# One more V tile kept between two attention layers, and the places at the change of layers dealt anew

## The chip, the core and the metric

The kernel runs on one core of a Trainium2 chip. The metric is the device time of one execution in microseconds (us). The engines named here: PE (matrix products), DVE (vector), ACT (activations), POOL (small extra vector work), SP (issues the loads), and the sixteen DMA engines that move the data. "1 MiB", "512 KB" and "256 KB" are sizes of one transfer; a tile of 1 MiB is 8 KB in each of the 128 partitions of the on-chip memory, and a *place* is half of a tile, 4 KB per partition.

## What is computed

Two identical rounds of attention and GLU for four single tokens, with the same weights and the same caches in both rounds:

```python
x = x + attn(layernorm(x), k_cache, v_cache, wq, wo)
x = x + glu(layernorm(x), w_gate, w_up, w_down)
x = x + attn(layernorm(x), k_cache, v_cache, wq, wo)
x = x + glu(layernorm(x), w_gate, w_up, w_down)

# attn: q = (x @ wq) in 32 heads of 128; 8 heads of K and V, last 2048 positions
#   p = softmax(q @ k.T * 128**-0.5); o = p @ v; return o @ wo
# glu: (sigmoid(x @ w_gate) * (x @ w_up)) @ w_down, 512 -> 1792 -> 512
```

Batch 4, width 512, everything bfloat16. K and V of the window have 16 MiB each, `wq` and `wo` 4 MiB each, the three GLU matrices 1.75 MiB each. The K cache stays on the chip after its first use; most of V and the weights except `wo` are read from HBM once per round.

## The kernel before, in words

**Memory.** One big array, `arena`, has 50 slots of 4 KB per partition. The first 32 hold K of all eight heads for the whole run. The other 18 are nine tiles of two slots, given out by a pool. V comes in 16 tiles of 1 MiB, one for each of 8 heads and each pair `bp` of batches. `wo` takes four tiles and stays until the second attention. So at the end of the first attention five tiles are left. Names in the code: `Y` = first V tile of head 7, `Z` = second V tile of head 7, `GA` = first V tile of head 6, `GB` = a pair of slots without content of its own. The fifth is the second V tile of head 6.

**What stays.** V of heads 7 and 6 is used last in the first attention and first in the second, where the heads run backwards. `Z` and the second tile of head 6 simply stay. `Y` is copied into four PSUM banks by four DVE transposes of 128x512 (`st0` to `st3`, line 574) and comes back by four transposes (`us0` to `us3`, line 589) into a tile that the second attention has freed. Half of `Z` goes to two more PSUM banks (`so0`, `so1`, line 596) and comes back into its place (`uo0`, `uo1`, line 602). Of `GA` one half stays (`KEPT`), the other half is loaded again.

**The ring of places.** At the change of layers the first GLU's weights (`wg`, `wu`: four transfers of 448 KB each; `wd`: three of 512 KB and one of 256 KB), then `wq` for the second attention (eight of 512 KB), then three V halves of 512 KB pass through six places: `GB` 0 and 1, `GA` 0, `Y` 0 and 1, `Z` 0. Each load names its place in a table written by hand (in `load_wq`, `load_glu`, `load_v`). A load waits until the matmul, or the transposes, that read the place before it have ended.

**Order.** The loads are issued by SP strictly in the order of the list `loads`; a load that waits holds up all behind it. For the other engines `_schedule` orders the operations before the run with a cost model: of those that could start within 60 ns of the earliest it takes the one written first. Each operation has the dependences that follow from what it reads and writes, from the PSUM banks it shares, and from explicit `after` and `deps`. From the second `wq` product on (`P.chain`) PE keeps the program's order.

**Units.** In the first attention, for each head: K is transposed in place (line 847), scores, softmax, probabilities transposed, two products with V (`pv_unit`, line 966), the rescaling `oe` (line 974), a permutation `pm` on PE (984), `oq` (989), and the product with `wo` (`wo_unit`, 1153), which adds up in PSUM bank `WB` over all heads. Then `attn_add` (1278) reduces that bank to the new x, and `layer_norm` (740 and following) begins with a sum over x (`ln_red`), a product that makes the mean (`ln_sum`), and the centred x (`ln_xn`). `glu` (1290) multiplies the `wg` and `wu` parts as they land (1330), transposes (1339), makes `hT` (1357) and multiplies the `wd` parts (1396). `q_second` and `q_mms` (788) do the second `wq` product in two halves (`i` = 1, then 0); the result of the first half is transposed (`qt1_1`, 800) and scaled (`qc1_1`, 804), and then unit 0 of the second attention starts with `qx2.0` (835) and its scores (865, 876). In the last GLU (`last=True`) the `wd` products are at line 1371, and four copies `oc0` to `oc3` (1382), by turns on ACT and DVE, bring the result into `ebuf`, from where it is stored.

## Time and profile before

| | us |
|---|---|
| median of three runs | 180.24 (179.0 to 181.01) |
| the profiled execution | 179.2 |
| its span, first to last instruction | 177.5 |
| busy: PE / DVE / ACT / POOL | 101.9 / 104.0 / 32.7 / 21.6 |
| DMA: bytes, mean rate over the span | 70.26 MB, 396 GB/s |
| V loads | 27 of 1 MiB, 3 of 512 KB |
| SP waiting for V products of line 966 | 27.5, in 8 waits |

Times in what follows are us from the first instruction of the span. In a row of a group or of the timeline the columns are start, length, engine, line, operation, what is written and read with partitions x elements, the count, and in brackets the idle time of the engine before it and what ended that. The chain that ended last goes back from the last instruction to what released each step. "DMA to landing" is the time from the start of an issue on SP until all sixteen engines have reported that transfer.

### The profile page before, as it was taken

To read this page: it belongs to the slowest core of one execution; us is meant where nothing else is said; L and a number is where in the kernel's file an instruction comes from. 1 tells how busy PE (TensorE), PEld (TensorE's weight loads), DVE (VectorE), ACT (ScalarE), POOL (GpSimd) and SP (SyncE) were. 2 spreads that over 40 slices of the span, in tenths; PEclk is the share of its full clock that TensorE was granted. 3 is DMA by queue.
4 is the path that set the end of the run, shared out by engine and by line. 5 is a ranking of instruction groups with operands and counts; after the bars stand their busy time and mean duration, and the time that the engine had idled before them with its cause. 6 is when DMAs were issued, how large, how long until landed. Compare 5 with 4: busy or idle time off the path is not lost.

```text
span 177.5 us, 3885 instructions
## 1 busy us (share of the span) xinstructions
PE 101.9 (57%) x1641; PEld 54.8 (31%) x1653; DVE 104.0 (59%) x256; ACT 32.7 (18%) x87; POOL 21.6 (12%) x88
## 2 busy tenths in 40 slices
PE   0635326481843635607417866456886999775763
PEld 0202102241431421503404852141323444435421
DVE  7308997838476374593473492332299999742341
ACT  2002031212030300300201101000043455430011
POOL 6100010101010100100100100000011453342000
PEclk9999999999999999999999999999999999975555
DMA  5999999999999999999999999999999999999990
GB/s 191 415 430 425 423 425 415 412 423 423 419 413 418 419 428 414 414 419 423 417 423 419 410 403 378 410 406 398 382 370 414 425 425 421 415 419 401 411 372 27
DMA packets 12738, 70.52 MB, mean 397 GB/s; under 512 B 1320, under 2 KB 1328, under 8 KB 6576
## 3 DMA queue, kind: packets, MB, share of 16 engines
q1 hardware_dynamic: 12712, 70.26, 97.1%
q8 instruction: 13, 0.21, 0.5%
q14 instruction: 5, 0.04, 0.1%
q10 hardware_dynamic: 8, 0.00, 0.0%
HBM read 70.26 MB, written 0.00 MB: 396 GB/s over the span
## 4 chain that ended last, share of the span: by engine, by line
DMA 35%; DVE 33%; PE 19%; issue 4%; SPq 4%; ACT 3%; POOL 1%; DVEq 0%; ACTq 0%
DMA arena<-in_A_v_cache_dram 15%; DMA arena<-in_B_w_down_dram 13%; DVE arena L847 11%; PE ps L876 7%; DVE nmax L889 5%; DMA arena<-in_A_wq_dram 4%; PE ps L966 4%; SPq L398 4%; DMA arena<-in_B_w_gate_dram 3%; PE ps L865 2%; DVE nmax L893 2%; DVE arena L1057 2%; DVE mxt L897 2%; DVE ebuf L924 2%; PE ps L1153 2%
## 5 line engine op out<-in xcount | busy, mean ns | idle before, releaser
L847 DVE STREAM_TRANSPOSE arena<-arena 128x1024 f32<-128x1024 f32 x32 | 37.0, 1202 | 0.0
L876 PE MATMUL ps<-arena,qbd 128*32 128x512 bf16 x256 | 25.6, 535 | 0.0
L889 DVE TENSOR_REDUCE nmax<-ps 128x1 f32<-128x512 f32 x16 | 10.8, 676 | 19.5 <-PE ps L876 19.3
L865 PE MATMUL ps<-msk_m,msk_s 128*32 128x512 bf16 x64 | 8.6, 526 | 23.2 <-DVE arena L847 21.8
L966 PE MATMUL ps<-ebuf,arena 128*128 128x8 bf16 x576 | 17.6, 168 | 7.4 <-DMA arena<-in_A_v_cache_dram 4.3
L966 PEld LDWEIGHTS ps<-ebuf,arena 128*128 128x128 bf16 x576 | 16.7, 104 | 9.3 <-DMA arena<-in_A_v_cache_dram 5.3
L904 ACT ACTIVATE prow<-ps,nmax 128x512 bf16<-128x512 f32 x16 | 11.0, 687 | 35.1 <-DVE nmax L901 29.5
L840 ACT CAST qbd<-ps 128x256 bf16<-128x256 f32 x16 | 5.9, 370 | 45.0 <-PE ps L876 35.1
L933 POOL CAST s<-psm 128x1 bf16<-128x1 f32 x9 | 1.7, 187 | 83.9 <-ACT prow L904 83.9
L876 PEld LDWEIGHTS ps<-arena,qbd 128*32 128x32 bf16 x256 | 8.4, 121 | 10.3 <-issue 7.7
L788 PE MATMUL ps<-arena,xn 128*4 128x512 bf16 x64 | 8.4, 572 | 5.4 <-DMA arena<-in_A_wq_dram 5.0
L919 ACT CAST prow<-ps 128x512 bf16<-128x512 f32 x16 | 9.4, 586 | 9.9 <-PE ps L966 2.1
L1330 PE MATMUL ps<-arena,xn 128*4 128x448 bf16 x64 | 7.7, 551 | 3.7 <-DMA arena<-in_B_w_up_dram 1.9
L924 DVE STREAM_TRANSPOSE ebuf<-prow 128x256 f32<-128x256 f32 x16 | 7.0, 435 | 3.8 <-ACT prow L919 3.7
L865 PEld LDWEIGHTS ps<-msk_m,msk_s 128*32 128x32 bf16 x64 | 1.7, 98 | 24.1 <-DVE arena L847 22.7
L800 DVE STREAM_TRANSPOSE ebuf<-ps 128x512 f32<-128x512 f32 x3 | 2.1, 717 | 10.6 <-PE ps L788 10.5
L766 ACT ACTIVATE lnv<-ps 128x4 f32<-128x4 f32 x4 | 0.7, 173 | 41.2 <-PE ps L762 41.2
L1048 PE MATMUL ps<-arena,ebuf 128*32 128x512 bf16 x112 | 7.9, 404 | 0.2 <-DVE nmax L901 0.2
L835 PE MATMUL ps<-qh,eyew 32*128 32x64 bf16 x64 | 5.6, 217 | 3.7 <-ACT qbd L840 2.4
L974 DVE TENSOR_TENSOR onb<-ps,rinv 128x16 bf16<-128x16 f32 x9 | 1.6, 182 | 9.5 <-PE ps L966 9.5
L1153 PE MATMUL ps<-onp,arena 128*128 128x16 bf16 x144 | 5.3, 175 | 2.7 <-DVE onp L989 2.4
L1339 DVE STREAM_TRANSPOSE ebuf<-ps 128x448 f32<-128x448 f32 x4 | 2.6, 649 | 6.6 <-PE ps L1330 6.6
(111 smaller groups left out, 131.8 us busy)
## 6 DMA issues: line engine op xcount, KB each, us to landing
arena<-in_A_v_cache_dram SPq DMA_DIRECT2D x27, 1024.0 KB, 22.4
arena<-in_A_k_cache_dram SPq DMA_DIRECT2D x16, 1024.0 KB, 25.2
arena<-in_A_wq_dram SPq DMA_DIRECT2D x4, 1024.0 KB, 7.9
arena<-in_A_wq_dram SPq DMA_DIRECT2D x8, 512.0 KB, 6.4
arena<-in_A_wo_dram SPq DMA_DIRECT2D x3, 1024.0 KB, 26.2
arena<-in_B_w_down_dram SPq DMA_DIRECT2D x4, 512.0 KB, 6.3
arena<-in_B_w_gate_dram SPq DMA_DIRECT2D x4, 448.0 KB, 8.5
arena<-in_B_w_up_dram SPq DMA_DIRECT2D x4, 448.0 KB, 5.4
```

Of the source, the lines that this page charges most:

```text
L788: last = pe.matmul(ps[32 * hh:32 * hh + NB, qb, :], xn[:, c * NB:(c + 1) * NB], src[:, o + hh * 512:o + (hh + 1) * 512], start=(c == 0), s ...
L847: P.op("vector", "T%d_%d" % (h, t), c_dve(1024), lambda v, v32=v32: v.transpose(v32, v32), r=[("slot", 4 * h + t)], w=[("slot", 4 * h + t)])
L865: last = pe.matmul(ps[32 * gi:32 * gi + 32, bank, :], msk_s[:, :], msk_m[:, :].unsqueeze(1).broadcast_to([128, 256, 2]), start=True, stop= ...
L876: last = pe.matmul(ps[32 * gi:32 * gi + 32, bank, :], qbd[:, q0:q0 + 32], kt[:, cp // 2, cp % 2, jh * NJ:(jh + 1) * NJ, :], start=False, s ...
L889: lambda v: v.tensor_reduce(nmax[:, k2:k2 + 1], ps[:, bank, :], AXX, ALU.max),
L904: lambda a: a.activation(prow[:, :].rearrange("p (m x t) -> p m x t", x=32, t=2), ps[:, bank, :].rearrange("p (m t x) -> p m x t", x=32, t ...
L919: P.op("scalar", "pc" + tag, c_act(512), lambda a: a.copy(prow[:, :], ps[:, pb, :]), r=[("ppb", pb)], w=[("prow",)], banks=(pb,))
L924: P.op("vector", "pt" + tag, c_dve(256), lambda v: v.transpose(et, prow[:, :].bitcast(F32)), r=[("prow",)], w=[("e", k2)])
L966: last = pe.matmul(ps[:, ob, bp * 8:bp * 8 + 8], src[:, j * 128:(j + 1) * 128], ev[:, j % 2, j % 16 // 2, x0:x0 + 8], start=(j == 0), stop ...
L1048: last = pe.matmul(ps[32 * g:32 * g + 32, ob, :], ew[:, g, mq, t], src.rearrange("p (m t d) -> p t m d", t=2, d=128)[:, t], start=(n == 0) ...
L1153: last = pe.matmul(ps[:, WB, c * NR:(c + 1) * NR], tile_ap(s)[:, o + r_ * D + c * 128:o + r_ * D + (c + 1) * 128], ov[:, r_ * NR:(r_ + 1) ...
L1330: last = pe.matmul(ps[32 * g:32 * g + NB, gub[n], 0:NF], xn[:, c * NB:(c + 1) * NB], slot_ap(s)[:, g * NF:(g + 1) * NF], start=(c == 0), s ...
```

## The change

One tile more stays: the first V tile of head 6 (formerly `GA`) is in `stay`, `KEPT` and its half load are gone, and that tile leaves the ring. The ring has five places: `GB` 0 and 1, `Y` 0 and 1, `Z` 0. All tables of places are dealt anew; `Z` 0 now carries one `wq` part as well, so `uo0` and `uo1` come after the third product of the `wq` half instead of the second. `st0` and `st1` must end before `oe` of head 6, `st2` and `st3` come between `oq` of head 6 and `oe` of head 7, `so0` between `oe` and `oq` of head 7, `so1` after that and before `ln_red`. The last `wo` part is loaded in two transfers and multiplied in two groups. The first norm of the GLU sums straight from PSUM, and `attn_add` runs behind that sum. The copies of the last GLU no longer claim the halves of `ebuf`. The stashed tile's return is placed after the first V load of round two instead of the second, since one load before it is gone.

```diff
-        GA = ("V", HKV - 2, 0, 0)
-        KEPT = ("kept",)
...
 # load_wq, places of (i = 0, i = 1):
-   (((Y, 1), (GB, 0), (GB, 1), (GA, 0)), ((GB, 0), (GB, 1), (GA, 0), (Y, 0)))[i][c])
+   (((GB, 1), (Y, 0), (Y, 1), (GB, 0)), ((Y, 0), (Y, 1), (Z, 0), (GB, 0)))[i][c])
...
 # load_wo, last pair:
-                for n in range(2):
-                    dma("wo%d" % (2 * hh + n), slot_ap(s + n), wo_d[:, 2 * hh + n, :], w=[("slot", s + n)], rate="bw_4k")
+                h = 2 * hh
+                dma("wo%d" % h, slot_ap(s), wo_d[:, h, :], w=[("slot", s)], rate="bw_4k")
+                n = REP * D // 2
+                a = dma("wo%da" % (h + 1), slot_ap(s + 1)[:, 0:n], wo_d[:, h + 1, 0:n], w=[("slot", s + 1)], rate="bw_4k")
+                b = dma("wo%db" % (h + 1), slot_ap(s + 1)[:, n:2 * n], wo_d[:, h + 1, n:2 * n], w=[("half",)], rate="bw_4k")
+                b.deps.update(a.deps)
...
 # load_glu: wg and wu, then wd
-   (((GB, 0), (GB, 1), (GA, 0), (Y, 0)), ((Y, 1), (Z, 0), (GB, 0), (GB, 1)))[nm == "wu"][c])
+   (((GB, 0), (GB, 1), (Y, 0), (Y, 1)), ((Z, 0), (GB, 0), (GB, 1), (Y, 0)))[nm == "wu"][c])
-   ((GA, 0), (Y, 0), (Y, 1), (Z, 0))[a // 4])
+   ((Y, 1), (Z, 0), (GB, 0), (GB, 1))[a // 4])
...
 # load_v
-   tiles = {(HKV - 2, 0): ((Y, 0),), (HKV - 3, 1): ((Y, 1), (GB, 0))}.get((h, bp)) if k else None
+   tiles = {(HKV - 3, 1): ((GB, 1), (Y, 0))}.get((h, bp)) if k else None
...
 # layer_norm
+            part, rd, bk, after = add or (xT[:, 0:NX], xts, (), None)
             P.op("vector", "ln_red" + tag, ds,
-                 lambda v: v.tensor_reduce(lnr[:, 0:nb], xT[:, 0:NX].rearrange("p (c b) -> p b c", c=NC), AXX, ALU.add),
-                 r=xts, w=[("lnr", 0)])
+                 lambda v: v.tensor_reduce(lnr[:, 0:nb], part.rearrange("p (n b) -> p b n", b=nb), AXX, ALU.add),
+                 r=rd, w=[("lnr", 0)], banks=bk)
+            if after is not None:
+                after()
...
 # q_second
             variance()
+            q_mms(1, 1, WB, (2,))
             unstash_half(())
-            q_mms(1, 1, WB, (2, 3))
+            q_mms(1, 1, WB, (3,))
...
 # attn_first
                 if h == HKV - 1:
-                    stash(stashed, (0, 1, 2))
+                    oe, oq = named("oe0.%d" % (h - 1)), named("oq0.%d" % (h - 1))
+                    oe[0].deps.add(stash(stashed, (0, 1)))
+                    st = stash(stashed, (2, 3), oq)
                     need(Z)
                 op = pv_unit(tag, h, h % 2, v_tiles[(0, h)])
                 if h == HKV - 1:
-                    st = stash(stashed, (3,), named("oe" + tag))
-                    named("oq" + tag)[0].deps.add(st)
-                    stash_half(0, "oq" + tag)
+                    oe, oq = named("oe" + tag), named("oq" + tag)
+                    oe[0].deps.add(st)
+                    oq[0].deps.add(stash_half(0, oe))
+                    so = stash_half(1, oq)
+                    give(base[Z])
...
 # last GLU, copies oc0 to oc3
-                         r=[("orow",)], w=[("oc", g), ("e", g // 2)], banks=() if g else (PBS[0],))
+                         r=[("orow",)], w=[("oc", g)], banks=() if g else (PBS[0],))
...
-        stay = keep[1:] + [(HKV - 2, 1)]
+        stay = keep[1:] + [(HKV - 2, 1), (HKV - 2, 0)]
...
-                    if n_v == cfg.get("ST", 2):
+                    if n_v == cfg.get("ST", 1):
...
-        attn_first()
-        attn_add(0)
-        glu(0, 0, NB)
+        so = attn_first()
+        n = len(P.ops)
+        glu(0, 0, NB, (ps[:, WB, 0:REP * NX], [("psw",)], (WB,), lambda: attn_add(0)))
+        P.ops[n].deps.add(so)
```

In `wo_unit` the last head's sixteen products become two operations of eight; the second waits for the second transfer:

```diff
+            half = REP // 2 if tag == "0.%d" % (HKV - 1) else REP
+            for r0 in range(0, REP, half):
...
-            P.op("tensor", "WO%s_%d" % (tag, h), NC * REP * tm["pe_pair"], e_wo,
-                 r=[("slot", s + h % 2)] + [("op", k2)], w=[("psw",)], banks=(WB,))
+                P.op("tensor", "WO%s_%d_%d" % (tag, h, r0), NC * half * tm["pe_pair"], e_wo,
+                     r=[("half",) if r0 else ("slot", s + h % 2)] + [("op", k2)], w=[("psw",)], banks=(WB,))
```

More of the change, by code (lines that the diff above doesn't have):

```diff
@@ L443, in take_load @@
             where[name] = s
-            if name in (Y, Z, GA, GB):
+            if name in (Y, Z, GB):
                 base[name] = s
@@ L592, in load_stash, with stash_half @@
             loads.append((name, emit))
-        def stash_half(n, name):
+        def stash_half(n, after):
             src = slot_ap(base[Z])[:, n * 1024:(n + 1) * 1024].bitcast(F32)
-            P.op("vector", "so%d" % n, c_dve(512), lambda v: v.transpose(ps[:, OBS[n], :], src),
-                 r=[("slot", base[Z])], w=[("so", n)], banks=(OBS[n],), after=[o for o in P.ops if o.name == name])
+            return P.op("vector", "so%d" % n, c_dve(512), lambda v: v.transpose(ps[:, OBS[n], :], src),
+                        r=[("slot", base[Z])], w=[("so", n)], banks=(OBS[n],), after=after)
         def unstash_half(after):
@@ L613, in load_v @@
                     halves[h, bp].append((half, 0))
-                if len(tiles) == 1:
-                    halves[h, bp].append((KEPT, 0))
                 return
@@ L620, in build @@
         on_free[Y] = lambda s: hfree.update((s, s + 1))
-        def keep_half(s):
-            hfree.add(s)
-            where[KEPT] = s + 1
-            left[KEPT] = 2
-        on_free[GA] = keep_half
         P.op("gpsimd", "ones", 200.0, lambda g: g.memset(ones_f[:], 1.0), w=[("ones_f",)])
@@ L728, in bview, with layer_norm @@
             return t.rearrange("p (c b) -> p c b", b=NB)[:, :, b0:b1]
-        def layer_norm(tag, b0, b1, for_q):
+        def layer_norm(tag, b0, b1, for_q, add=None):
             ds = tm["dve_small"]
@@ L1147, in wo_unit, with e_wo @@
             o = h % 2 * REP * D
-            def e_wo(pe):
-                last = None
-                for r_ in range(REP):
-                    for c in range(NC):
-                        last = pe.matmul(ps[:, WB, c * NR:(c + 1) * NR],
-                                         tile_ap(s)[:, o + r_ * D + c * 128:o + r_ * D + (c + 1) * 128],
-                                         ov[:, r_ * NR:(r_ + 1) * NR], start=(first and r_ == 0 and c == 0),
-                                         stop=(final and r_ == REP - 1), skip_group_check=True)
-                return last
-            P.op("tensor", "WO%s_%d" % (tag, h), NC * REP * tm["pe_pair"], e_wo,
-                 r=[("slot", s + h % 2)] + [("op", k2)], w=[("psw",)], banks=(WB,))
+            half = REP // 2 if tag == "0.%d" % (HKV - 1) else REP
+            for r0 in range(0, REP, half):
+                def e_wo(pe, r0=r0):
+                    last = None
+                    for r_ in range(r0, r0 + half):
+                        for c in range(NC):
+                            last = pe.matmul(ps[:, WB, c * NR:(c + 1) * NR],
+                                             tile_ap(s)[:, o + r_ * D + c * 128:o + r_ * D + (c + 1) * 128],
+                                             ov[:, r_ * NR:(r_ + 1) * NR], start=(first and r_ == 0 and c == 0),
+                                             stop=(final and r_ == REP - 1), skip_group_check=True)
+                    return last
+                P.op("tensor", "WO%s_%d_%d" % (tag, h, r0), NC * half * tm["pe_pair"], e_wo,
+                     r=[("half",) if r0 else ("slot", s + h % 2)] + [("op", k2)], w=[("psw",)], banks=(WB,))
             done(name)
@@ L1184, in attn_first @@
                 wo_unit(tag, h, op, h % 2, False, h == HKV - 1)
+            return so
         def attn_second():
@@ L1288, in attn_add, with glu @@
                  r=[("x2",)] + [("xT", b) for b in range(NB)], w=[("xT", b) for b in range(NB)])
-        def glu(k, b0, b1, last=False):
+        def glu(k, b0, b1, add=None, last=False):
             nb = b1 - b0
-            variance = layer_norm("G%d" % k, b0, b1, False)
-            if k == 0:
-                stash_half(1, "ln_redG0")
-                give(base[Z])
+            variance = layer_norm("G%d" % k, b0, b1, False, add)
             gub = OBS
@@ L1453, in build @@
         attn_add(2)
-        glu(1, 0, NB, True)
+        glu(1, 0, NB, last=True)
         assert not loads
```

## The prediction, written before the changed kernel ran

> **What bounds the kernel now.** I read four views in this order: the queue part of the page, the chain that ended last, the DMA issues with their time to landing, and the end of TensorE's timeline.
>
> ```profile
> DMA  5999999999999999999999999999999999999990
> GB/s 191 415 430 425 423 425 415 412 423 423 419 413 418 419 428 414 414 419 423 417 423 419 410 403 378 410 406 398 382 370 414 425 425 421 415 419 401 411 372 27
> ...
> q1 hardware_dynamic: 12712, 70.26, 97.1%
> ```
>
> The sixteen DMA engines are busy in every slice but the first and last. Only slices 24 to 29 (106 to 133 us) sink to 370-410 GB/s. That is the change of layers, the stretch that the diff deals anew.
>
> ```profile
> 101.18 1.58 PE ps L966 x60
> 102.76 6.09 DMA arena<-in_B_w_gate_dram
> ...
> 110.87 6.27 DMA arena<-in_B_w_down_dram
> 117.14 0.05 issue
> 117.19 0.60 PE ps L1396 x16
> 117.79 0.02 issue
> 117.81 6.81 DMA arena<-in_A_wq_dram
> 124.62 0.04 issue
> 124.66 0.59 PE ps L788 x4
> ```
>
> This is the chain inside 98-127 us. It runs through the ring of places: a matmul frees a place, its new transfer lands 6.1 to 6.8 us later, the next matmul frees the next place. After 124.66 the page's chain stays with PE and DVE until 156.82: the second attention runs at its own pace, not at that of the transfers.
>
> ```profile
> DMA to landing us min/median/max: 4.7/6.4/11.6
> ```
>
> That is the answer for the load issues (L398) from 95 to 135 us. It holds queueing, so the minimum, not the median, is what a transfer needs.
>
> ```profile
> 170.02 0.92 PE L1330 MATMUL ps<-arena,xn 128*4 128x448 bf16 x8 [0.42 <-DMA arena<-in_B_w_up_dram]
> 170.72 0.64 PE L1315 MATMUL ps<-prow,xT 128*4 128x128 f32 x8
> 172.51 1.02 PE L1371 MATMUL ps<-arena,hT 128*4 128x128 bf16 x32 [1.14 <-DMA arena<-in_B_w_down_dram]
> 173.76 1.01 PE L1371 MATMUL ps<-arena,hT 128*4 128x128 bf16 x24 [0.23 <-DMA arena<-in_B_w_down_dram]
> ```
>
> The end waits for the last `wd` parts (landings at 172.46, 173.72 and 174.35). So both count: when the stream ends, and whether the second attention lets the last GLU start in time.
>
> **The change, part by part.** Landing times below are the sixteenth update of each transfer's semaphore.
>
> *One transfer less.* V of head 6, first half of its batches, was loaded again in one 512 KB half; now all of it stays. In this stretch 512 KB landings follow each other by 1.27 to 1.28 us. Term: **-1.27** on the stream.
>
> *Last output weights in two.* One 512 KB transfer becomes two of 256 KB with 2 KB rows. The one 256 KB transfer of the stretch (last `wd` of layer 1) landed 0.67 after its forerunner: 2 x 0.67 - 1.27 = **+0.07**. The additional issue costs SP 0.43 us (the row of the `wo` issues), with `wg` waiting behind it; `wg` 0 is issued at 96.9 instead of 96.49 and lands at 105.51, hidden by the queue. The product in two groups of 8 is the same 0.59 us of PE.
>
> A rule speaks against that split: the Trainium skill, "DMA: Bandwidth & Descriptors", section "Bandwidth", wants transfers batched to 1 MiB or more, and the fit in its section "Anatomy of one DMA" (2.0 us plus the bytes at 436 GB/s, measured on another issue path) would make two transfers of 256 KB dearer by 2.0 us than one of 512 KB and turn the whole sum to about +0.9. In this trace transfers stand in a queue and the fixed part does not show: 2.49 us for 1 MiB, 1.28 for half, 0.67 for a quarter.
>
> *Transposes of the kept tile forward.* `st0`, `st1` now precede `oe0.6`. Their tile landed at 99.31 while DVE idled from 99.21 to 100.65; two at 0.70 end at 100.7, so `oe0.6` slips 0.05. `st2`, `st3` follow `oq0.6`, `so0` follows `oe0.7`, `so1` follows `oq0.7`. If PE keeps its order, `so1` ends at 104.95; if the planner puts the seventh head's product ahead of `pm0.6`, at 105.2. The second half of Z, hence its first place, is then free at about 105 instead of 106.40. `ln_red` reads PSUM (0.23, the row of L1278; 0.18 if as cheap as L740) and the addition runs beside the 0.59 us mean. `xn` comes at 105.85 to 106.1 instead of 106.31. Worth nothing at the end: from `wg` 2 (lands 107.73) on the GLU waits for landings. Without this cover it would be worth 0.2 to 0.5 either way.
>
> *Five places instead of six.* I walked through the ring by hand: place free, issue, previous landing. The distance from an issue to the previous landing is the time the queue has before it runs dry. Now it is 4.4 to 5.5 us mostly, and 3.57 and 3.87 at `wu` 1 and 2, which landed on time (steps 1.10 and 1.13 where 1.12 is the norm). With five:
> - `wg` 2 goes to Y, free after head 7's first product: issue 101.5 to 102.0, distance 4.6 to 5.1; `wg` 3 102.8 to 103.4, 4.3 to 4.9; `wu` 0 104.95 to 105.2, 3.6 to 3.9.
> - `wu` 1, 2 after `wg` 0, 1: 106.5 and 107.2, 3.5 and 3.9. `wu` 3 after `wg` 2: 108.36, 3.9. `wd` 0 to 3: 109.48, 110.88, 111.72, 112.85; 3.8, 3.7, 4.1, 4.3.
> - `wq` second half: 113.95, 115.61 (after the first `wd` product, which waits for `hT`), 116.53, 117.81; 3.9, 3.5, 4.3, 4.3. First half: 118.25, 120.30, 121.48, 124.03; 5.1, 4.3, 4.4, 3.1. The last reuses the place of the fourth second-half part.
> - V head 5: 125.31 and 126.66, 3.1 and 3.0; then the first full V at 128.37 and the next at 130.84, both after K tiles of the second attention, about 2.6 each.
>
> What does an issue need? At `wu` 1 the first engine finished 2.88 after the issue, 1.12 of it transfer: 1.76. At the V issued at 130.84 (first landing 136.77, transfer 2.49) it was 3.45, though that engine was free 0.13 earlier. So between 1.8 and 3.5. At 1.8 nothing starves. At 3.5, walking through again, `wu` 1 slips 0.2 and the rest holds until the V transfers; there the second full V ends at 130.84 + 3.45 + 2.49 = 136.8 plus the engines' spread of 0.3, still over a microsecond before today's 138.50. I take 0.1 (nearer to `wu` 1 itself, same size and place) on what lands up to `wq`, bounds 0 and 0.4: **+0.10**.
>
> *Places given back later.* `uo0`, `uo1` (L602, 0.70 and 0.71) run at 118.58 and 119.93 now, beside the norm. Their place now holds the third `wq` part, so they start after its matmul at 122.72 and end near 124.1. Behind them on DVE stands `qt1_1` (L800, at 124.04), and behind that `qc1_1`, `qx2.0`, the scores: **+0.10**; bounds 0 (planner puts `uo1` behind) and 0.7 (both slip by a transpose). `q1_0_0` needs that bank free: 124.66, half a microsecond later.
>
> *The last four copies.* Each wrote a token of its half of `ebuf` as well as its own, so DVE's first copy waits for ACT's first and its second for ACT's second:
>
> ```profile
> 174.83 0.54 ACT L1382 CAST ebuf<-ps 4x128 bf16<-4x128 f32 x2 [5.10 <-PE ps L1371]
> 175.11 0.60 DVE L1382 CAST ebuf<-ps 4x128 bf16<-4x128 f32 x2 [3.22 <-ACT ebuf L1382]
> ```
>
> Without that token both engines start at 174.83 and DVE ends at 175.43 instead of 175.71. They overlap for one copy already, at 0.26 and 0.28 each, so I see no price. Nothing lies beside it: **-0.28**, whatever else happens (0 if the two slow each other).
>
> *Nobody else.* POOL and ACT get no further instruction; `ST` counts one load less, so the stashed tile still returns after head 5's half.
>
> **Sum.** The second attention starts 0.07 + 0.10 + 0.10 = 0.27 late and, being its own bound, ends 0.27 late. Then, at today's durations: `wg` products until 168.23; `wu` no longer waits (its last landing 169.98 - 1.2), ends 170.47 instead of 170.94; transpose 0.65 behind the reciprocal (ends 170.51) and `hT` at 171.47; 1.02 + 0.6 + 0.41 of `wd` products give 173.55, against 174.80 now. With 0.27: 173.8. The stream alone: 174.35 - 1.20 + 0.10 = 173.25, last product 173.7. Both ends agree on 1.0 us less, and 0.28 of copies makes it **1.3**. The profiled execution took 179.2 (span 177.5 + 1.7), so 177.9 for one like it. The three runs shown have a median of 180.24; the gain lies in stages that every run has, so I forecast 180.24 - 1.3 = **178.9**, minus 0.7%. A measurement here tells from no change about 1%: this is within it.
>
> **Rivals.**
> 1. *The ring turns too slowly: slower.* Six places x 1.28 = 7.7 us is today's turn: 6.4 to landing plus 0.6 of matmul plus waits. If those 6.4 were real latency and not queueing, five places would still take 7.5 us for 6.4 us of stream and lose 1.1 per turn. 23 transfers are 4.6 turns: 5.1 lost, 1.2 and 0.28 saved, 183.9. With 1.1 us of use, a turn outgrows the stream from 5.3 us to landing upward, outweighs the saving from 5.6 and costs over 1% from 6.0. For it: no landing in steady flow under 5.0 but one. Against it: that one, 4.67, landed without delay, and at 6.3 the queue held three to four transfers.
> 2. *The saving comes back as a later second attention: no change.* Its start hangs on `wq`, `qt1_1` and DVE order. If the slips reach their bounds, 0.07 + 0.4 + 0.7 = 1.2, only the copies' 0.28 is left: 180.0. For it: the chain from 124.66 to 156.82 has no DMA in it. Against: the slips need the planner to choose badly.
> 3. *More than the stream: faster by over 1%.* The slow slices hold landings late by 0.43, 0.45, 0.36, 0.12 and 0.40 beyond their sizes, 1.76 in all. Half of it gone with the halved V transfer (0.45 was its own), plus the earlier norm, gives 180.24 - 1.3 - 0.9 = 178.0. Against: compute would have to be earlier too, and nothing before `wq` is taken away.
> 4. *It does not do what it says*: if the tile stayed but another load took its bytes, 70.26 MB would remain; the load list gives 12.0 instead of 12.5 MiB of V. No share.
>
> **How the numbers follow.** Forecast 0.62 (178.3 to 179.5), rival 1 0.13, rival 2 0.13, rival 3 0.12. Own runs differ by 1.1%, so the range reaches from 177.7 (most of rival 3) to 181.0 (rival 2 and slips between it and rival 1) and leaves out rival 1 at its price and a little at the lower end. Faster by over 1%: rival 3 and the fast edge of the forecast, 0.22. Slower: rival 1 and what goes wrong beyond rival 2, 0.17. The rest 0.61.
>
> **What would show it.** Queue bytes 69.74 MB. `st` at 99.4, `so1` ended by 105.3, `uo` at 122.7, `qt1_1` within 0.2 of today's time. Landings of 512 KB V: two, not three. Time to landing of `wu`, `wd`, `wq` near 5 instead of 6.3 with the same steps of 1.28; if it stays at 6.3 and the steps widen, rival 1 is right. Last `wd` 1.0 to 1.2 earlier with `hT` just ahead of it; DVE's copies at the end starting with ACT's. I am wrong if GB/s in slices 24 to 29 falls below 370, or if the planner moves a wait into the second attention's chain.

## The result, and the profile after

The changed kernel is **slower**: 181.60 us median of six runs (181.15 to 182.24), beside 179.65 (178.65 to 181.01) for the kernel before, a ratio of **1.0101** with a 95% interval of 1.0062 to 1.0140. The forecast was 178.9 with a range to 181.0. The profiled execution after took 181.15 us with a span of 179.4; before it was 179.2 and 177.5.

The queue part of the page of the changed kernel, over the whole span in 40 slices:

```profile
DMA  5999999999999999999999999999999999999990
GB/s 184 431 426 424 422 426 409 416 422 422 420 415 420 418 420 426 411 422 420 418 424 422 396 375 353 395 322 408 348 258 420 422 426 416 418 417 403 413 369 28
...
q1 hardware_dynamic: 12712, 69.74, 96.5%
```

The bytes went down as they should, 70.26 to 69.74 MB. But slices 24 to 29, at the change of layers, now read 353, 395, 322, 408, 348 and 258 GB/s, where they read 370 to 410. The prediction named "below 370" there as the sign that it was wrong. The row of tenths still shows 9 throughout: it cannot show a dry spell (a time in which the queue holds too little to keep all sixteen engines at work) of one microsecond.

The chain that ended last, changed kernel, between 98 and 131 us (start, length, what):

```profile
104.73 0.74 DVE ps L598
105.56 0.24 DVE lnr L735
105.84 0.60 PE ps L740 x2
106.47 0.17 DVE xn L743
106.64 0.09 DVE xT L747
106.73 0.05 issue
106.79 0.94 PE ps L1332 x8
107.75 5.37 DMA arena<-in_B_w_up_dram
113.17 0.57 PE ps L1332 x3
113.76 4.90 DMA arena<-in_B_w_down_dram
118.66 0.05 issue
118.71 0.39 PE ps L1398 x8
119.11 7.13 DMA arena<-in_A_wq_dram
126.29 0.60 PE ps L785 x4
...
128.31 1.73 PE ps L874 x16
130.06 0.70 DVE nmax L887
```

Before, the chain's transfers were those of `wg`, `wd` and `wq`. Now one of `wu` takes the place of `wg`, behind the norm and the first `wg` product. The chain's `wq` transfer, the first part of the second half (called `wq0_0` in what follows), ends at 126.24 instead of 124.62. The scores that release the next places end at 130.04 instead of 128.35. So the change of layers is 1.6 us late where the prediction had it 0.27 late.

The busy times of each engine in three stretches of the changed kernel (last three columns: granted clock, DMA share, GB/s); before, the last two read 1.01 and 387, 1.01 and 397, 1.04 and 379:

```profile
107.00:113.00 6.00, 3.40 (x26) 0.89 (x18) 1.73 (x5) 0.72 (x4) 0.00 (x0) 1.00 0.92 348
119.00:125.00 6.00, 2.98 (x19) 1.30 (x16) 1.56 (x7) 0.38 (x2) 0.00 (x0) 1.00 0.99 367
125.00:131.00 6.00, 5.23 (x48) 1.68 (x52) 2.55 (x7) 0.74 (x2) 0.00 (x0) 1.00 0.91 330
```

The clock is 1.00 in all of them, so TensorE's speed is no part of it. The first stretch is `wu`. Its second part (`wu` 1; parts are counted from 0) was issued at 107.38, and it landed at 112.02, 2.14 us after its forerunner, where 1.12 is the norm and 1.10 was measured before. This distance from one landing to the next is called a *step* in what follows. The first engine had its share of `wu` 1 at 110.60 and the sixteenth at 112.02. Of the forerunner they had theirs at 108.47 and 109.88, so the two landings were 1.41 us apart already; if they are the same two engines, each lost about 1.0 us. The next large gaps are at the second `wq` part (step 2.45, where 1.28 is the norm for 512 KB) and around the scores: two V halves with steps of 2.43 and 2.02, then the first whole V tile, issued at 130.06 and landed at 137.72, 3.29 us after its forerunner, where 2.49 is the norm for 1 MiB.

The gaps are not all idle time. Of the packets of 3.5 KB that began between 108 and 110 us in the changed kernel, seven took 0.49 to 0.96 us, where the median is 0.14; before, the longest of that stretch took 0.32. Of the first ten packets of the first whole V tile, eight took 1.28 to 2.08 us, where the median is 0.31; before, two took 1.96 and 2.18. Why they take so long is not known.

The end of the timeline, changed kernel:

```profile
174.75 1.02 PE L1373 MATMUL ps<-arena,hT 128*4 128x128 bf16 x32 [1.15 <-DMA arena<-in_B_w_down_dram]
...
176.00 1.02 PE L1373 MATMUL ps<-arena,hT 128*4 128x128 bf16 x24 [0.23 <-DMA arena<-in_B_w_down_dram]
...
177.07 0.54 ACT L1384 CAST ebuf<-ps 4x128 bf16<-4x128 f32 x2 [5.12 <-PE ps L1373]
177.08 0.61 DVE L1384 CAST ebuf<-ps 4x128 bf16<-4x128 f32 x2 [2.94 <-PE ps L1373]
177.76 0.35 SPq L398 DMA_DIRECT2D out_dram<-ebuf  x1
```

The last products still wait for the last `wd` parts, which land at 176.60 instead of 174.35. The copies start together, and from the last landing to the issue of the output it is 1.16 us, before 1.44: that part of the prediction came as worked out.

### The profile page after: what moved, and what is told of

The parts are those of the page before. It is cut to its first block, busy times and chain, and to the rows that moved or that the text cites. A ratio compares the mean times of both kernels' runs of the same rounds, so it can differ in the third digit from the quotient of the medians.

```text
span 179.4 us, 3902 instructions
## 1 busy us (share of the span) xinstructions
PE 106.8 (60%) x1653; PEld 54.9 (31%) x1653; DVE 104.3 (58%) x256; ACT 32.7 (18%) x87; POOL 21.6 (12%) x88
## 3 DMA queue, kind: packets, MB, share of 16 engines
q1 hardware_dynamic: 12712, 69.74, 96.5%
## 4 chain that ended last, share of the span: by engine, by line
DVE 34%; DMA 34%; PE 20%; SPq 4%; issue 3%; ACT 3%; POOL 1%; DVEq 0%; ACTq 0%
DMA arena<-in_A_v_cache_dram 15%; DMA arena<-in_B_w_down_dram 12%; DVE arena L845 11%; PE ps L874 7%; DVE nmax L887 5%; DMA arena<-in_A_wq_dram 4%; SPq L398 4%; PE ps L964 3%; DMA arena<-in_B_w_up_dram 3%; PE ps L863 2%; DVE nmax L891 2%; DVE arena L1055 2%; PE ps L915 2%; DVE mxt L895 2%; DVE ebuf L922 2%
## 5 line engine op out<-in xcount | busy, mean ns | idle before, releaser
L915 PE MATMUL ps<-prow,perm 128*128 128x512 bf16 x16 | 8.2, 510 | 7.8 <-ACT prow L902 7.8
```

Of the source, the lines that this page charges most:

```text
L915: lambda pe: pe.matmul(ps[:, pb, :], perm[:, :], prow[:, :], start=True, stop=True),
```

## The experiments

In all of them "before" is the kernel before, run on the same chip. A landing is the sixteenth update of a transfer's semaphore, as in the prediction. The diffs are against the kernel named. "Six places" means the old tables of places; it needs half of `GA`'s tile, so that only the other half can be kept. In runs "without the reload" that other half is used for both halves in the second attention (a part of the result is then not the reference's), so that the bytes are those of the changed kernel. The first theory was: the other edits are worth what the prediction says, and the loss of the sixth place costs about 2 us.

### The parts of the change, one by one

**The copies alone**, against before:

```diff
-                         r=[("orow",)], w=[("oc", g), ("e", g // 2)], banks=() if g else (PBS[0],))
+                         r=[("orow",)], w=[("oc", g)], banks=() if g else (PBS[0],))
```

> The kernel before with the last four copies freed of each other and nothing else. If DVE's wait for ACT is all there is at that place: 0.28 us less than before (the row of L1382: 175.11 becomes 174.83), with every landing unchanged. If two engines that read one PSUM bank slow each other: 0.

Measured: ratio 0.9986 (0.9938 to 1.0034). In its profile the last landing and the output's issue are 1.17 us apart. The 0.28 us are there in the trace and too small for the measured times to show.

**Every edit but the place**, against after:

```diff
+        GA = ("V", HKV - 2, 0, 0)
+        KEPT = ("kept",)
...
 # load_wq, load_glu, load_v: the tables of places of the kernel before
 # q_second: uo0 and uo1 right behind the norm again; ST is 2 again
...
-        stay = keep[1:] + [(HKV - 2, 1), (HKV - 2, 0)]
+        stay = keep[1:] + [(HKV - 2, 1)]
```

> All other edits of the change (transposes forward, last output weights in two, norm from PSUM, copies) with the six places, the half kept and the half loaded again as before. Place theory (the lost sixth place lets the queue run dry): no widened steps, 0.2 to 0.5 us less than before, the first up-weight of place Z issued near 105.5 and no 2.1 us step behind it. Edits theory (the moved transposes and the split cost it): about 2 us more than before, as the changed kernel.

Measured: 0.9973 (0.9935 to 1.0010). The earlier transposes, the norm from PSUM, the split of `wo` and the copies do no harm; a gain of a quarter of a per cent is possible and not shown.

**The same without the reload**, against the kernel just above:

```diff
 # load_v
+            if k and (h, bp) == (HKV - 2, 0):
+                halves[h, bp] = [(KEPT, 0), (KEPT, 0)]
+                return
-            tiles = {(HKV - 2, 0): ((Y, 0),), (HKV - 3, 1): ((Y, 1), (GB, 0))}.get((h, bp)) if k else None
+            tiles = {(HKV - 3, 1): ((Y, 1), (GB, 0))}.get((h, bp)) if k else None
```

> As six_edits, but the half of V that was loaded again is not loaded: 512 KB less, six places. The second attention uses the kept half of that tile twice, so that part of the computation is not the reference's. Stream theory (the kernel is bound by its bytes): 1.2 us less than six_edits, in all about 1.5 us less than before. Release theory (the first whole V tiles of round two are issued only when the scores give K tiles free, at 128.4 and 130.8, and land 7.2 to 7.7 us later in both kernels, so bytes ahead of them save nothing): at most 0.4 us less than six_edits.

Measured: 0.9987 (0.9956 to 1.0019). This is the change's saving without its price, and no gain is left: 512 KB less, the same time. The 0.67% that 1.2 us would be, counted from the run above (0.9906), lies outside the interval. Against this run, with the same bytes, the changed kernel is 1.14% slower (1.0101 / 0.9987). That is the price of the sixth place, about 2.05 us, together with the later `uo0` and `uo1`, which are back in their old order in this run.

### Where the sixth place is missed

**Sixth place once, for the second `wu` part**, against after (the half of `GA` serves `wu` 1, and `wu` 2 and 3 move up by one place; from `wd` on each load waits for the same product as in the changed kernel; without the reload):

```diff
 # load_glu: wu, wd
-   ((Z, 0), (GB, 0), (GB, 1), (Y, 0))
+   ((Z, 0), (GA, 0), (GB, 0), (GB, 1))
-   ((Y, 1), (Z, 0), (GB, 0), (GB, 1))[a // 4]
+   ((Y, 1), (Z, 0), (GA, 0), (GB, 0))[a // 4]
...
```

> The changed kernel, but the second up-weight part goes to a sixth place, the first half of the V tile of head 6, which stands free since that tile's first product; the two behind it move up one place, and from the first down-weight on every load waits for the same matmul as in the changed kernel. The second attention uses the other half of that V tile twice, so that part of the computation is not the reference's. Place theory: the step of 2.14 us at the second up-weight goes back to 1.1, the step of 2.45 at the second query weight stays, the query products come 0.9 to 1.0 us earlier than in the changed kernel, and the time is about 0.9 us less than it. If the first dry spell only delays what a later one would delay anyway: under 0.3 us.

Measured: 1.0065 (1.0029 to 1.0100), 0.36% or 0.65 us better than the changed kernel, between the two expectations; the intervals overlap, so the gain is not clear of noise. The second part lands on time now (111.00, step 1.09), but the third, issued at 107.43, has a step of 1.57. The dry spell moved by one transfer and shrank to 0.45. The step of 2.45 at the second `wq` part stayed, as expected.

**Sixth place later, from the first `wd` part on**, against after (the complement, without the reload):

```diff
 # load_glu: wd
-   ((Y, 1), (Z, 0), (GB, 0), (GB, 1))[a // 4]
+   ((GA, 0), (Y, 1), (Z, 0), (GB, 0))[a // 4]
 # load_wq: six places as well; uo0 and uo1 again right behind the norm
```

> The complement of the run that gave the sixth place to the second up-weight alone: the changed kernel with five places up to the fourth up-weight, and the sixth place (half of the first V tile of head 6) in the ring from the first down-weight on. The kept other half of that tile is used for both halves in the second attention (that part of the output is not the reference's; no byte more is loaded than in the changed kernel). Places theory, by its two shares: the dry spell at the second up-weight stays (step 2.1 us instead of 1.1), the one from the down-weights on goes; six places throughout were 1.14% faster than the changed kernel and the place for the second up-weight alone 0.36%, so this one should be some 0.8% faster than the changed kernel, ratio to the kernel before 0.999 to 1.005, 180.0 to 181.0 us. Rival, that the first dry spell is the cause and all later ones follow from it: no better than the changed kernel, ratio 1.008 to 1.012. Second rival, that the shares do not add up because any one gap delays the first whole V load alike: ratio 1.005 to 1.008.

Measured: 1.0103 (1.0066 to 1.0141). The two shares do not add up; my expectation fell, and the value is that of its first rival. The sixth place shows no gain once `wu` has been late. In its profile `wu` 1 has a step of 2.68. The windows of this kernel, in the same columns as above:

```profile
107.00:113.00 6.00, 3.07 (x26) 0.89 (x18) 1.59 (x4) 0.72 (x4) 0.00 (x0) 1.00 0.97 347
119.00:125.00 6.00, 3.89 (x37) 1.81 (x33) 2.18 (x8) 0.38 (x2) 0.00 (x0) 1.00 1.01 369
125.00:131.00 6.00, 5.16 (x52) 1.60 (x52) 2.01 (x6) 0.74 (x2) 0.00 (x0) 1.00 0.92 343
```

The first stretch is as poor as with five places, 347 GB/s, and the others get little from the additional place. The DMA share in it is 0.97 all the same: the engines were busy, but with longer packets.

**Only the issue of `wu` 1 late**, against before (six places, all bytes, old copies; the load waits for the first `wg` product although its place is free):

```diff
+                    if (nm, k, c) == ("wg", 0, 0):
+                        [o for o in P.ops if o.name == str(("wu", 1, 0))][0].deps.add(P.ops[-1])
```

> The kernel before with one wait more: the load of the second up-weight part also waits for the first product of the first GLU, as it does in the changed kernel; the six places stay. It is then issued near 107.2 instead of 106.4, 2.8 us before the previous landing instead of 3.6. If the last engine needs 3.5 us from issue to start: its step grows from 1.10 to about 1.8, everything behind it comes 0.7 us later, and the time grows by 0.5 to 0.7 us (0.3 to 0.4%). If 1.8 us are enough, as I took it blind: no change in the step and the time.

Measured: 1.0052 (1.0018 to 1.0086). An issue at 107.11 instead of 106.42 costs half a per cent. (SP issues in order, so the next two go out late as well: 107.48 and 107.95 instead of 107.22 and 107.59.) But not where I expected it: `wu` 1 itself landed at 111.01 with a step of 1.12; `wu` 3 had 2.02 and the first `wq` part 2.93. So there is no fixed time from an issue to its start that separates on time from late: this transfer needed less than 2.8 us, and `wu` 3, two behind it, issued at 107.95 with its forerunner landing 4.1 us later, came 0.9 us late.

### Why the saved bytes were worth nothing

The first whole V tile (head 5) has a place only when the scores of unit 0 have read the K tile there. In every profile in which it is one transfer it is issued 3.6 to 4.2 us after `wq0_0` has landed, lands 6.8 to 8.0 us after that, and the stream ends 38.2 to 39.7 us later. The half that is no longer loaded stood in the list *behind* `wq0_0`. If this chain sets the end, its bytes lay in the time that the queue spends waiting for the scores anyway.

**Less left for the scores to release**, against six places without the reload (the first half of the first whole V tile gets a place of the ring, only the second half waits for the scores):

```diff
 # load_v
+            if k and (h, bp) == (HKV - 3, 0):
+                ...
+                load_half(names[0], src[:, :, 0:SLOT], "bw_4k", SLOT, (GB, 0))
+                load_stash(("V",) + keep[0] + (1,))
+                load(names[1], 1, "bw_4k", (SLOT, src[:, :, SLOT:2 * SLOT], True))
+                ...
-            tiles = {(HKV - 3, 1): ((Y, 1), (GB, 0))}.get((h, bp)) if k else None
+            tiles = {(HKV - 3, 1): ((Y, 0), (Y, 1))}.get((h, bp)) if k else None
```

> six_no_reload with the places after the query weights dealt one earlier: the halves of V head 5, second batches, take the place that the missing load left and the next, and the first half of V head 5, first batches, takes the third, so that of that tile only 512 KB wait for the scores of unit 0. The second attention again uses one half of V of head 6 twice in place of the other, so that part of the computation is not the reference's. Release theory (the end follows the landing of the first loads that wait for K tiles; saved bytes count only if less is left to start there): the last half lands about 1.3 us earlier than the whole tile did, and the time is 1.0 to 1.3 us less than six_edits. If saved bytes are worth nothing at all here: as six_no_reload, about the time of before.

Measured: 0.9917 (0.9878 to 0.9957), 0.7% or 1.3 us below the kernel without the shift (the two intervals just touch): about the whole saving that the prediction had counted. The second half, issued at 128.01, landed at 133.25, where the whole tile had landed at 136.79; 0.93 us of that is `wq0_0`, which landed earlier in this execution. The stashed tile's return moves along and still comes directly ahead of what waits for the scores. It needs the sixth place and the left-out half at once, so it is no kernel that computes the reference.

**The same 512 KB ahead of `wq0_0`, or behind it.** Both are the kernel with six places and without the reload, plus one transfer: the output weights of head 0, loaded again into their own place. No place of the ring is taken. Only the position differs:

```diff
 # first run
         load_glu(0)
+        loads.append((("K", "extra"), lambda _: dma("wox", slot_ap(where["wo", 0]), wo_d[:, 0, :],
+                                                    w=[("slot", where["wo", 0])], rate="bw_4k")))
         load_wq(1)
 # second run: the same lines behind load_wq(1)
```

> The kernel with six places and no half loaded again (the kept half used for both halves, as there), and one transfer of 512 KB more: the output weights of head 0, loaded again into their own place right after the first GLU's last weights, ahead of the second query weights. Nothing waits for it and it holds no place of the ring. In all profiles so far the first whole V load is issued 5.0 to 5.5 us after the fourth query part of the first half has landed (123.35 and 128.37 before, 124.98 and 130.06 after the change), and the stream's end follows that load by 38.3 to 39.7. Chain theory: 512 KB ahead of that query part delays it by 1.2 to 1.3 us, and with it the end by 0.9 to 1.3: ratio to the kernel before 1.004 to 1.008 (without the transfer it was 0.9987), 180.3 to 181.0 us. Rival, that the end follows the bytes of the whole stream: as the kernel before, whose bytes it has, 0.996 to 1.000. Second rival, that a fuller queue removes dry spells for as much as the bytes cost: 0.996 to 1.001 too, with no step over 1.4 us between 106 and 125 us.

> The same kernel with the same 512 KB transfer, only placed behind all second query weights instead of ahead of them. Chain theory: it lies in the time that the queue spends waiting for the first whole V load's release, and costs nothing: ratio 0.996 to 1.000, and 0.5 to 0.9% less than the same transfer ahead. Rival, the bytes of the whole stream: the same as the kernel with the transfer ahead, within 0.3%.

Measured: 1.0080 (1.0046 to 1.0114) ahead, 0.9986 (0.9941 to 1.0031) behind. The intervals do not overlap. **512 KB behind that point costs nothing that shows, ahead of it 0.94% (1.7 us).** That is at the upper edge of what was expected, and more than the 1.28 us of the transfer; the two profiles differ by less, 0.73 us at the last landing. The chain that ended last, first the kernel with the transfer ahead, then the one with it behind:

```profile
117.95 7.72 DMA arena<-in_A_wq_dram
125.67 0.04 issue
125.72 0.60 PE ps L796 x4
...
127.69 1.69 PE ps L884 x15
```

```profile
117.86 6.96 DMA arena<-in_A_wq_dram
124.82 0.04 issue
124.87 0.59 PE ps L796 x3
...
126.83 1.62 PE ps L884 x15
```

The `wq` transfer of the chain lands 0.85 us later in the first. The "behind" run had lost 0.6 us at the second `wq` part (step 1.87) in this execution, and the other 0.13 (step 1.41); without these the distance would be 0.85 + 0.59 - 0.13 = 1.3, the 1.28 of the transfer.

**Scores earlier**, against every edit but the place (full computation; the mask product ahead of the last part of the first query half, the second unit's queries ahead of the first unit's scores):

```diff
+            P.op("tensor", "M2.0", 4 * tm["pe_row"], e_m0, r=[("msk_s",), ("msk_m",)], w=[("pss", 2)], banks=(OBS[0],))
+            q_mms(1, 1, WB, (3,))
...
-            score(0, lambda: q_mms(1, 0, OBS[1], (1,)))
-            qx(1)
+            def before_s0():
+                q_mms(1, 0, OBS[1], (1,))
+                qx(1)
+            score(0, before_s0)
```

> A real candidate: all edits of the change but the place (six places, half of the first V tile of head 6 loaded again), and in addition the mask product of the second attention's first unit ahead of the fourth part of the second query product, and the second unit's queries ahead of the first unit's scores. Same computation, same bytes as before. If the end follows the issue of the first whole V load, which waits for the first unit's scores, these end some 0.2 us earlier and the second unit's 0.5 earlier, and the kernel is 0.2 to 0.4 us faster than the same without the shift (ratio to the kernel before 0.9975 before, so 0.993 to 0.997). Rival, that the end follows the bytes of the stream: nothing, ratio 0.996 to 0.999.

Measured: 1.0016 (0.9978 to 1.0053). The edit missed its aim. TensorE's timeline in this kernel:

```profile
125.83 0.60 PE L795 MATMUL ps<-arena,xn 128*4 128x512 bf16 x4 [0.43 <-DMA arena<-in_A_wq_dram]
126.36 0.39 PE L852 MATMUL ps<-qh,eyew 32*128 32x64 bf16 x4
126.68 1.90 PE L893 MATMUL ps<-arena,qbd 128*32 128x512 bf16 x16
```

The scores now stand behind the second unit's queries, in an order that PE may not change, and the product ahead of both waits for its weights until 125.79. They start at 126.68 instead of 126.38. The first whole V was issued at 128.63 instead of 128.24 and landed at 135.74 instead of 135.10, and the stream ended at 174.23 instead of 173.86. So it is no test of earlier scores; the delay of 0.39 us at the issue is 0.37 at the stream's end in these two executions.

**The released tiles in halves.** I had also suspected that a transfer of 1 MiB starts more slowly on a queue that is running dry. The first two released V tiles were loaded as two transfers of 512 KB each, once with six places and the reload, once in the changed kernel:

```diff
 # load_v
+            if k and (h, bp) in ((HKV - 3, 0), (HKV - 4, 1)):
+                ...
+                    for n in range(2):
+                        dma("%s_%d" % (name, n), slot_ap(s + n), pair_d(A_v, h, bp)[:, :, n * SLOT:(n + 1) * SLOT],
+                            w=[("slot", s + n)], rate="bw_4k")
```

> six_edits, and the two V tiles that are issued when the first scores give K tiles free (head 5 first batches, head 4 second batches) are loaded in two transfers of 512 KB instead of one of 1 MiB. If a transfer of 1 MiB takes longer to get going on an almost empty queue than one of half (issue to landing less its own 2.49 us is 4.4 to 5.5, against 3.1 to 4.6 for the halves before it): the tile lands 0.5 to 1.0 us earlier, and the time is 0.5 to 1.0 us below six_edits. If the start does not depend on the size: as six_edits, or 0.1 more for the two additional issues.

> The changed kernel with the same two V tiles in halves. If the slow start of those tiles is part of what it loses: 0.5 to 1.0 us less than the changed kernel, and still slower than before, since the dry spell at the second up-weight (a step of 2.1 us) is untouched. If its loss comes all from the late start of the second attention: as the changed kernel.

Measured: 0.9995 (0.9957 to 1.0033) and 1.0174 (1.0130 to 1.0218). The suspicion fell: no gain with six places, and 0.7% worse than the changed kernel with five (the intervals still overlap). In the profile of the second run, though, the loss is there before the split transfers are issued (`wu` 2 lands at 114.28 instead of 113.12, `wq0_0` at 128.13 instead of 126.24). Why an edit further down should make the first turn worse, I cannot say.

### The chain in all profiles

Landings and the issue in us, one execution each; the first whole V tile is V5. "Half" marks the run in which only its second half waits for the scores, "halves" those in which it is two transfers that both wait.

| kernel | `wu` 1 landed | `wq0_0` landed | V5 issued | V5 landed | last `wd` landed | ratio |
|---|---|---|---|---|---|---|
| before | 111.09 | 124.62 | 128.37 | 135.61 | 174.35 | 1 |
| the copies alone | 111.06 | 124.81 | 128.57 | 136.20 | 174.66 | 0.9986 |
| every edit but the place | 111.16 | 124.66 | 128.24 | 135.10 | 173.86 | 0.9973 |
| scores earlier | 111.26 | 124.42 | 128.63 | 135.74 | 174.23 | 1.0016 |
| six places, tiles in halves | 111.16 | 124.38 | 128.68, 129.26 halves | 135.83 | 176.04 | 0.9995 |
| without the reload | 111.02 | 125.06 | 128.81 | 136.79 | 175.13 | 0.9987 |
| less left for the scores | 111.03 | 124.13 | 128.01 half | 133.25 | 173.29 | 0.9917 |
| 512 KB behind | 111.07 | 124.82 | 128.48 | 136.31 | 174.77 | 0.9986 |
| 512 KB ahead | 111.19 | 125.67 | 129.40 | 137.28 | 175.50 | 1.0080 |
| issue of `wu` 1 late | 111.01 | 126.42 | 130.18 | 137.67 | 177.01 | 1.0052 |
| sixth place once | 111.00 | 125.70 | 129.54 | 136.32 | 176.01 | 1.0065 |
| sixth place later | 112.58 | 125.75 | 129.86 | 137.65 | 176.63 | 1.0103 |
| after | 112.02 | 126.24 | 130.06 | 137.72 | 176.60 | 1.0101 |
| after, tiles in halves | 111.72 | 128.13 | 131.82, 132.40 halves | 139.98 | 179.72 | 1.0174 |

Single executions of one kernel scatter by about 1%, so neighbours in the table may change places. But two groups show: with `wq0_0` by 125.1 the last landing comes by 175.2, with `wq0_0` at 125.6 or later it comes at 175.5 to 179.7. One profile does not fit: six places with the tiles in halves, 124.38 and 176.04, though its measured ratio is that of the first group.

## Why the prediction was wrong, point by point

**"One transfer less: -1.27 on the stream" is the first step that failed.** The bytes went, and the time did not come back. It assumed that the stream's end follows the sum of its bytes. But the stream has a release in its middle: the first whole V tile waits for scores, which wait for the query product of `wq0_0`. What is taken away behind `wq0_0` only lengthens the wait. The runs show it from both sides: nothing without the reload, nothing for 512 KB put back behind, 0.94% for the same 512 KB ahead, and 0.7% when less was left for the scores to release. The view that could have told was there: the chain of before runs from the `wq` landing at 124.62 through the scores to 128.37, and the slices around it were the slow ones. I read that chain as the pace of the second attention alone, and my walk had the two full V tiles land over a microsecond early only because it put the engines' spread at 0.3 us. Before, the second of them, issued at 130.84, landed on its first engine at 136.77 and on its last at 138.50, 1.73 us apart: issue, start and spread already gave the landing that was there, and nothing was left to gain at it. After, V5 landed on its first engine 5.9 us after the issue and on its last 7.7.

**"Five places instead of six: +0.10" is the second, and the larger one.** It measured about 2.05 us, far above its upper bound of 0.4. Three things were wrong in it. The need of an issue, 1.76 us, was read from the engine that is done first, but the time at hand was counted to the landing of the forerunner on the engine that is done last. The first engine has its share up to 2.0 us sooner (107.96 against 109.99 at `wu` 0 before), so it runs dry long before the walk says so: after the change it had 1.09 us, from the issue at 107.38 to 108.47, against 1.54 before. The issue itself was put at 106.5, although my own estimate had the centred x at 105.85 to 106.1, and one further vector operation and a product of half a microsecond come before the place is free: it was 107.38, only 2.5 us ahead of the landing of its forerunner, not 3.5. And the walk let a late transfer delay only itself and its successors by the same amount, while the run with one late issue shows new gaps behind a transfer that was in time. The walk's conclusion that "`wu` 1 slips 0.2 and the rest holds" became 0.93 at `wu` 1 and 1.62 at `wq0_0`. Of the difference 0.75 is the second `wq` part (step 2.45, before 1.70); how much of that is this execution's alone is not known (below). Together the two steps account for the miss: 1.27 that did not come and 1.95 too little for the place are 3.2 us, and between the forecast's -1.3 and the measured +1.8 lie 3.1.

**What held.** The copies: -0.28 in the trace. The last `wo` part in two: landings 0.67 apart twice. The Trainium skill, "DMA: Bandwidth & Descriptors", section "Bandwidth", wants transfers of 1 MiB or more; in this full queue the trace does not agree, with 0.67 us for 256 KB and 1.28 for 512 KB, and the kernel with that split and six places is not slower. `uo0` and `uo1` ahead of the query transpose, in DVE's timeline of the changed kernel:

```profile
124.39 1.47 DVE L604 STREAM_TRANSPOSE arena<-ps 128x512 f32<-128x512 f32 x2 [3.53 <-PE ps L785]
125.78 0.67 DVE L797 STREAM_TRANSPOSE ebuf<-ps 128x512 f32<-128x512 f32 x1
```

The transpose of the queries starts at 125.78, and its product ended at 125.62 (start 125.02, 0.60 long), so the two cost 0.16 where 0.10 was set. The issue of V5 follows `wq0_0` by 3.82 us, before 3.75, so little of that reached the scores. The transposes forward and the norm from PSUM: `so1` ended at 105.46 (105.3 foretold) and the centred x came at 106.47 instead of 106.31, 0.4 to 0.6 later than worked out. In the sum that term was nothing, because the GLU waits for landings. With five places it is not nothing: the place of `wu` 1 depends on that norm.

**The rivals.** Rival 1, the ring that turns too slowly, was right in sign and in cause, and wrong in price: 1.8 us came, it said 3.7. It counted 1.1 us lost in every turn. The runs show that the first turn matters most: with six places from `wd` on nothing was gained. Its predicted sign was a time to landing that stays at 6.3 while the steps widen; the forecast's own was a time near 5 with the same steps. The answer for the load issues from 95 to 135 us in the changed kernel:

```profile
DMA to landing us min/median/max: 4.3/6.1/9.9
```

The median sank only from 6.4 to 6.1, and the steps widened: that is nearly the rival's sign and not the forecast's. Rival 2 had the right place, a second attention that starts late, but the slip came with the transfers and not through the order on DVE. Rivals 3 and 4 are out: the slow slices got slower, and the bytes went as the change says. The prediction's estimate of about +0.9 for a dearer split leaves out the copies; with them it would be about +0.7.

**The sum as it came**, in the two profiles: `wq0_0` +1.62, from there to the issue of V5 +0.07, its landing +0.42, the rest of the stream +0.14, the copies -0.28, together +1.97 at the issue of the output (177.76 against 175.79).

**What stays open.** Why the sixth place at `wu` 1 alone wins back only about a third of the loss, if that, while at all later places it wins nothing; why the first packets behind a gap take several times as long as the others; why the engines' landings of one transfer lie up to 2 us apart; why tiles in halves made the first turn worse; and what makes the second `wq` part slow in some executions. No kernel with the reference's result was clearly faster than before; the best is the one with every edit but the place, whose interval still touches 1.

## What to carry to other kernels

Before a saved transfer is booked as time, look in the list of loads for the next one that waits for a computed result, and ask whether the saved bytes stand ahead of what that result needs or behind it; behind, they are worth nothing until that wait is shortened. When buffers are taken from a ring, walk through it with the need and the time at hand of the same engine, and count every operation up to the release: here one issue 0.7 us later cost half a per cent, and places added after the first turn behind a dependence (a norm) won nothing. A sum whose only large gain and only large risk sit in the same stretch should be measured there first with the edits apart.

## What the runs showed of the hardware that I had not expected

- **The sixteen engines are far apart, and the first packets behind a gap are slow.** In the full queue, at 87 to 105 us before the change, the first and the last engine had their shares of one transfer 1.9 to 2.0 us apart. At the changed kernel's `wu` 1 it was 1.4, at V5 1.75. The first packet of V5 began 1.64 us after the start of the issue, and its early packets took up to 2.08 us where 0.31 is the median. The Trainium skill, "DMA: Bandwidth & Descriptors", section "Latency and other measured facts", gives about 0.6 us to the first byte for transfers issued this way. Here the first load of an execution, on an empty queue, began its first packet 1.04 us after the start of its issue (before), and the issue itself took 0.41 us of that, so counted from its end the trace agrees. The time until a whole transfer has landed is another matter: from the start of the issue, 3.9 us was the least for 448 KB at the change of layers (`wu` 1 in the run in which it is issued late).
- **Late issues need not hurt themselves.** With `wu` 1 issued 0.7 us late it landed on time, and steps of 2.02 and 2.93 us came two and seven transfers later (during the second of them an instruction fetch was on, see the next point).
- **Code loading uses the same engines.** The instruction queue of the changed kernel's page:

```profile
q8 instruction: 13, 0.21, 0.5%
```

Its packets are of 16 KB and hold one DMA engine for about 1.0 us each. One of them comes at 118.3 to 119.9 us in every profile here. The second `wq` part, which is on its way then, had steps from 1.11 to 2.99 us, where 1.28 is undisturbed: before 1.70, after 2.45, with 512 KB ahead 1.41. But with every edit but the place the fetch came at 118.76 and the step was 1.26. So the fetch alone does not make the difference, and no run takes it away.
